# Weight gradients of half the tokens moved beside the forward, kept as fp32 partial sums in DRAM; row sums of a shift gradient as matmuls

## The chip, the cores and the metric

The kernel runs on one core of one Trainium2 chip. The metric is the device time of one execution in microseconds, the median over runs. The engines are TensorE (PE; its weight loads are shown apart as PEld), VectorE (DVE), ScalarE (ACT), GpSimd (POOL) and SyncE (SP, which here only issues DMAs and DMA transposes).

## The reference

One transformer block with adaptive layer norm, forward and backward, on 2048 tokens of width D = 512 (32 heads of 16, MLP width F = 1792), in bf16. Besides the output, the gradients of x, of all weights and of the conditioning vector c are returned.

```python
mod = silu(c) @ w_mod                      # six rows of 512: sa, ca, ga, sb, cb, gb
h = layernorm(x) * (1 + ca) + sa
x = x + ga * attention(h, wqkv, wo)        # full softmax, 32 heads
h = layernorm(x) * (1 + cb) + sb
x = x + gb * (relu(h @ w1 + b1)**2 @ w2 + b2)
out, vjp = jax.vjp(f, x, wqkv, wo, w1, b1, w2, b2, c, w_mod);  grads = vjp(grad_out)
```

The parts that matter here are dW1 = h^T du and dW2 = a^T (gb * g), where du is the gradient at the MLP's first product, a the squared relu and g the output's gradient, and the sums that feed the gradients of cb, sb and gb: products of the unscaled weight gradients with w1 and w2, summed, and db1 @ w1^T for sb.

## The kernel before

The tokens are handled in four chunks of 512 (`SC = 4`), the width of the MLP in 14 tiles of 128 (`FT`), D in four of 128 (`DT`), and the tokens in 16 tiles of 128 (`ST`). The work goes in this order:

1. An opening (`gen_open`, `gen_qkv`) up to 275 us: layer norm, QKV, and the attention of chunk 0.
2. `fwd_rest` (275 to 984 us): the attention of chunks 1 to 3, eight head groups each, 16 key blocks to a group, 384 steps in all. A step has four score matmuls, two exponentials of 128x1024 on ACT and 16 small matmuls into the accumulators. Behind it a `Background` runs generators: `gen_mlp(sc)` is the output projection, the MLP forward and the MLP backward down to dO of chunk `sc`, and it is added to the queue when the attention of that chunk is done. `bg.burst(rate, ...)` gives it a number of units a step (a unit is a matmul of 512 columns); a burst ends where a PSUM tile is finished (`stopped`), and `("wait", n)` lets n/2 steps pass. Slots that are not used are filled by dummy matmuls (line 520).
3. `last_chunk` (984 to 1179 us): the MLP of chunk 3 forward and backward, then both weight gradients over all 16 token tiles. `gen_dw1` makes dW1 in 14 tiles of 64 matmuls with 128 columns, `gen_dw2` makes dW2 in 14 tiles of 16 matmuls with 512 columns. Both need `du` and `a` with tokens on the partitions: for the first three chunks these come by DMA transpose from DRAM (`duT_d`, `aT_d`, written by `gen_mlp`), for the last one from SBUF (`turned`: tiles `tm_blk` and `tm_l`). They are generators as well, and `fill.take(n)` puts n units of them between the steps of the last chunk; the loads for the attention's backward are issued on SP between the units of `gen_dw2`, from its mark `half` on.
4. `attn_bwd` and `phase6` (1179 us to the end): the backward of the attention, and the remaining weight gradients.

PE and SP run in the order of the program. DVE, ACT and POOL are ordered by the compiler's planner in stages 2 and 3. PSUM has eight banks; in `fwd_rest` the background has one (`mps`), in `last_chunk` the gradients have three (`dps`), transposes two (`tps`), everything else three.

In `gen_dw1` DVE makes three passes over each tile piece: the scaled output (line 1110), the product with w1 for cb (line 1112), and the product of `csb` with w1 for sb (line 1115); `csb` is db1 in a row, spread over the partitions by a matmul of ones with a diagonal (lines 1101 to 1103). The marks `fc2_0` to `fc2_2` say how far a chunk's generator has come; `phase_fwd` runs the generator of chunk 2 up to its mark before the last chunk begins, and the rest of it is taken in pieces by `last_chunk` (`bg.take`, `bg.drain`).

## Time and profile before

| what | value |
|---|---|
| median of 3 runs | 2525.01 us (2522.04 to 2526.73) |
| the profiled execution | 2527.3 us, span 2525.3 us |
| granted TensorE clock, mean | 0.994 |
| PE, DVE, ACT, POOL busy | 96%, 67%, 90%, 28% of the span |
| moved by DMA | 454 MB |

A row of groups reads: line, engine, operation, the tile written and the tiles read, the shapes, the count; then the total busy time in us and the mean of one in ns; then the engine's idle time just before them and what ended most of it. A row of the timeline or of the chain starts with the start and the duration in us. A row of stages starts with the stretch, its length, and the busy time (with the count) of PE, PEld, DVE, ACT and POOL, then the granted clock, the busy share of the DMA engines and GB/s. SPq is the queue of SP.

### The profile page before, as it was taken

The page shows a single profiled execution, that of the slowest core. Times are in us where ns is not written, and L with a number is a line of the kernel's source. Part 1 is how long each engine was busy: PE and PEld are TensorE (multiplying, and loading weights), DVE is VectorE, ACT ScalarE, POOL GpSimd, SP SyncE. Part 2 cuts the span into 40 slices and gives each one's busy share as a digit, 9 for nine tenths or more (in the row PEclk, how much of TensorE's full clock was granted, in tenths as well). Part 3 has the DMA queues.
Part 4 walks back from the last instruction along what each step waited for, and adds up shares of the span by engine and source line. Part 5 has one row for each costly group of instructions (what it writes and reads, how often), then busy time and mean ns, then how long its engine had stood idle before and what let it go on. Part 6 is the DMA issues. An engine that isn't in the chain of part 4 may idle for free.

```text
span 2525.3 us, 69141 instructions
## 1 busy us (share of the span) xinstructions
PE 2424.0 (96%) x26994; PEld 1032.7 (41%) x27199; DVE 1683.0 (67%) x3343; ACT 2283.0 (90%) x3757; POOL 715.7 (28%) x1265
## 2 busy tenths in 40 slices
PE   8999999999999999989999999999999999999988
PEld 4555444545554544573232333332333333333333
DVE  6222212322342333576999999999999999999857
ACT  7999999999999996533999999999999999999934
POOL 2344430120121021246222332322332323222323
PEclk9999999999999999999999999999999999999999
DMA  4689650451244054599999999999999999999997
GB/s 166 133 179 209 162 124 22 127 118 48 99 103 100 22 145 120 111 188 214 236 237 226 233 237 232 236 226 228 230 233 234 233 234 234 239 227 238 241 179 188
DMA packets 1291630, 454.19 MB, mean 180 GB/s; under 512 B 1235796, under 2 KB 1260246, under 8 KB 1291302
## 3 DMA queue, kind: packets, MB, share of 16 engines
q1 hardware_dynamic: 1252422, 344.68, 72.4%
q0 software_dynamic: 36800, 104.04, 14.1%
q8 instruction: 212, 3.47, 0.6%
q10 hardware_dynamic: 2080, 1.05, 0.2%
q14 instruction: 116, 0.95, 0.1%
HBM read 75.83 MB, written 64.49 MB: 56 GB/s over the span
## 4 chain that ended last, share of the span: by engine, by line
PE 40%; ACT 8%; DMA 8%; issue 2%; DVE 2%; POOL 0%; SPq 0%; DVEq 0%; ACTq 0%; POOLq 0%
PE st L1710 16%; PE acckv L1561 8%; ACT pu L1713 6%; PE accq L1586 5%; DMA dsT<-ds 4%; PE dps L1151 2%; PE dp L1624 2%; DMA keep<-ds 1%; DMA dqT<-dq_t 1%; ACT csq L1642 1%; PE st L1856 1%; DVE ds L1628 1%; PE dp L1761 1%; PE st L1667 1%; PE st L1574 1%
## 5 line engine op out<-in xcount | busy, mean ns | idle before, releaser
L1628 DVE TENSOR_TENSOR ds<-dp,pu 128x512 bf16<-128x512 f32 x1888 | 1166.8, 684 | 36.5 <-PE dp L1624 20.6
L1713 ACT ACTIVATE pu<-st 128x512 bf16<-128x512 f32 x2048 | 1073.6, 666 | 37.2 <-PE st L1710 21.3
L507 ACT ACTIVATE pu<-st 128x1024 bf16<-128x1024 f32 x768 | 704.9, 1127 | 6.0 <-PE st L503 5.6
L1624 PE MATMUL dp<-kvm,q 64*128 64x512 bf16 x1024 | 364.0, 383 | 2.1 <-DVE ds L1628 1.0
L1624 PE MATMUL dp<-kvm,dOTg 64*128 64x512 bf16 x1024 | 364.9, 384 | 1.0 <-DVE ds L1628 0.8
L1710 PE MATMUL st<-kvm,QTg 64*128 64x512 bf16 x1024 | 348.8, 382 | 6.0
L1710 PE MATMUL st<-kvm,q 64*128 64x512 bf16 x1024 | 347.9, 381 | 5.1 <-ACT pu L1713 0.2
L1643 POOL TENSOR_TENSOR ds<-csq,pu 128x512 bf16<-128x512 f32 x128 | 147.2, 1150 | 626.5 <-ACT csq L1642 547.4
L482 PEld LDWEIGHTS <-pu 128*128 128x128 bf16 x6144 | 216.5, 96 | 158.0 <-issue 83.2
L482 PE MATMUL accbank<-Vaug,pu 128*128 128x17 bf16 x6144 | 265.2, 172 | 10.1 <-ACT pu L507 7.4
L520 PE MATMUL st<-QTm,KTq 128*128 128x512 bf16 x670 | 202.7, 379 | 6.3 <-ACT pu L507 2.7
L413 ACT ACTIVATE pu<-st 128x1024 bf16<-128x1024 f32 x224 | 206.6, 1060 | 2.3 <-PE st L410 1.9
L503 PE MATMUL st<-QTm,KTq 32*128 32x512 bf16 x1536 | 171.9, 385 | 5.2 <-issue 1.0
L1561 PE MATMUL acckv<-ds,Qg 128*16 128x512 bf16 x1024 | 176.5, 383 | 0.2
L1561 PE MATMUL acckv<-pu,dOg 128*16 128x512 bf16 x1024 | 176.4, 383 | 0.0
L1561 PE MATMUL acckv<-ds,q 128*16 128x512 bf16 x1024 | 175.8, 382 | 0.0
L1561 PE MATMUL acckv<-pu,q 128*16 128x512 bf16 x1024 | 175.8, 382 | 0.0
L410 PE MATMUL st<-QTm,KTq 128*128 128x512 bf16 x435 | 130.0, 377 | 10.1 <-ACT pu L413 4.0
L1710 PEld LDWEIGHTS <-q 64*128 64x128 bf16 x1024 | 66.9, 94 | 162.9 <-issue 150.0
L1710 PEld LDWEIGHTS <-QTg 64*128 64x128 bf16 x1024 | 67.1, 94 | 161.5 <-issue 146.5
L347 PEld LDWEIGHTS <-pu 128*128 128x128 bf16 x2048 | 86.4, 96 | 59.6 <-issue 3.0
L1624 PEld LDWEIGHTS <-q 64*128 64x128 bf16 x1024 | 88.8, 93 | 51.3 <-issue 40.8
(399 smaller groups left out, 3365.7 us busy)
## 6 DMA issues: line engine op xcount, KB each, us to landing
KTq<-KTq_d POOLq DMA_DIRECT2D x24, 512.0 KB, 3.8
duT_d<-auT POOLq DMA_DIRECT2D x3, 1792.0 KB, 7.3
aT_d<-rT POOLq DMA_DIRECT2D x3, 1792.0 KB, 11.9
KTq_d<-KTq SPq DMA_DIRECT2D x32, 128.0 KB, 2.2
QTq_d<-ev_fm SPq DMA_DIRECT2D x32, 128.0 KB, 4.4
ktm_d<-ev_tm POOLq DMA_DIRECT2D x32, 128.0 KB, 2.6
VTq_d<-vT POOLq DMA_DIRECT2D x4, 1024.0 KB, 6.1
dx<-dx_d SPq DMA_DIRECT2D x16, 256.0 KB, 4.6
```

The source lines that it names most:

```text
L410: nc.tensor.matmul(stt[:, a, :], lhsT=KT[:, kb * P:(kb + 1) * P], rhs=QTm[2 * jp + a][:], start=True, stop=True)
L413: nc.scalar.activation(pu[:], stt[:], ACT.Exp, scale=self.scale)
L482: nc.tensor.matmul(acc[:, j, sub, :], lhsT=pus[half][:, a, sub * P:(sub + 1) * P], rhs=Vaug[:, kb, 4 * g + j, :], start=(kb == 0 and j == ...
L503: nc.tensor.matmul(tiles[h // 2][:, h % 2, :], lhsT=KT[r, kb * P:(kb + 1) * P], rhs=QTm[g % 2][r, :], start=True, stop=True)
L507: nc.scalar.activation(pu[:], t[:], ACT.Exp, scale=self.scale)
L520: nc.tensor.matmul(tiles[0][:, 0, :], lhsT=KT[:, 0:P], rhs=QTm[g % 2][:], start=True, stop=True)
L1561: nc.tensor.matmul(acckv[r:r + DH, :], lhsT=T[n][:, ib, col:col + DH], rhs=src[:, a, :], start=(ib == 0), stop=(ib == ST - 1))
L1624: nc.tensor.matmul(dp[:], lhsT=T["dOT"][rd, ib * P:(ib + 1) * P], rhs=masked["VT"][a][rd, 512 * c:512 * (c + 1)], start=True, stop=True)
L1628: nc.vector.tensor_tensor(dsg[:, i, a], dp[:], pu[:, a, :], ALU.mult)
L1643: nc.gpsimd.tensor_tensor(dsg[:, i, 1], f[:], pu[:, 1, :], ALU.mult)
L1710: nc.tensor.matmul(stt[:], lhsT=T["QT"][rs, q], rhs=masked["KT"][a][rs, c0:c0 + 512], start=True, stop=True)
L1713: nc.scalar.activation(pu[:, a, :], stt[:], ACT.Exp, scale=self.scale)
```

## The change

The weight gradients of chunks 0 and 1 (`SE` = 8 token tiles) move into the background of the forward. The generator of chunk 1 makes them for chunk 0, that of chunk 2 for chunk 1: `gen_dw2_early` ahead of the first fc2 tile, `gen_dw1_early` behind the second. Each makes 14 tiles of 128x512 from four token tiles. Chunk 0's sums are stored to `dw2p_d` and `dw1p_d` in fp32; chunk 1's passes load them, add, and store again, and the last w1 pass also takes the products with w1 and scales the sum. Buffers are the former `auT` (operand of 4 token tiles, four sums) and the free `QTm[2]`, `QTm[3]`. The rate of the background goes from 3 to 4 units a step, and the mark `fc2_{sc}` moves from behind the first fc2 tile to behind the third. `gen_dw1` and `gen_dw2` then run over the other eight token tiles and add the partial sums: on POOL in the first, on DVE in the second. The row sums for sb become matmuls: each w1 block is transposed on PE, copied by ACT, and multiplied with db1, split into three bf16 parts, into one PSUM tile that stays open for all 14 tiles.

```diff
@@ fwd_rest
-                done = 0 if ... else bg.burst(3.0, self, most)
+                done = 0 if ... else bg.burst(4.0, self, most)
@@ last_chunk
-        xh2 = e0.tile([P, ST, D], BF16, name="xh2")
+        xh2 = e0.tile([P, ST - self.SE, D], BF16, name="xh2")
@@ turned
-            r = pool.tile([P, ST - 4, P], BF16, name="tm_blk", bufs=4)
-            nc.sync.dma_start_transpose(r[:], src_d[ft, :, :(ST - 4) * P])
+            r = pool.tile([P, ST - 4 - SE, P], BF16, name="tm_blk", bufs=4)
+            nc.sync.dma_start_transpose(r[:], src_d[ft, :, SE * P:(ST - 4) * P])
@@ gen_dw1
+        rows = self.dps.tile([P, 512], F32, name="dps")
+        def add_rows(ft):
+            nc.tensor.matmul(rows[0:32, :], lhsT=db1s[:, ft, :], rhs=turnedw[ft][:], start=(ft == 0), stop=(ft == FT - 1))
 ...
-                nc.gpsimd.dma_start(w[:], w1_v[:, :, ft * P:(ft + 1) * P])
+                nc.sync.dma_start(w[:], w1_v[:, :, ft * P:(ft + 1) * P])
+            part = sb.tile([P, DT, P], F32, name="part1", bufs=3)
+            nc.sync.dma_start(part[:].rearrange("p a b -> p (a b)"), self.dw1p_d[ft])
 ...
-                for st in range(ST):
+                for st in range(SE, ST):
 ...
+            tp = self.tps.tile([P, DT, P], BF16, name="tp")
+            for kt in range(DT):
+                nc.tensor.transpose(tp[:, kt, :], w1_blk[:, kt, :], self.ident[:])
+            turnedw.append(sb.tile([P, D], BF16, name="w1T", bufs=2))
+            nc.scalar.copy(turnedw[ft][:], tp[:].rearrange("p a b -> p (a b)"))
+            if ft:
+                add_rows(ft - 1)
             csb_ps = ...
-            dw1 = sb.tile([P, DT, P], BF16, name="dw1")
+            dw1 = sb.tile([P, DT, P], BF16, name="dw1", bufs=3)
             for kt in range(DT):
                 nc.scalar.activation(t1[:, kt, :], csb[:], ACT.Copy, scale=self.mod_col(3)[:, kt:kt + 1])
+            nc.gpsimd.tensor_tensor(t1[:], t1[:], part[:], ALU.add)
+            for kt in range(DT):
 ...
-                nc.vector.scalar_tensor_tensor(junk2[:], csb[:], 1.0, w1_blk[:, kt, :], ...)
@@ gen_dw2
+            part = sb.tile([P, D], F32, name="part2", bufs=4)
+            nc.sync.dma_start(part[:], self.dw2p_d[ft])
 ...
+            nc.vector.tensor_tensor(part[:], pt[:], part[:], ALU.add)
-            nc.vector.tensor_tensor(dw2[:], pt[:], self.mod_row(5), ALU.mult)
+            nc.vector.tensor_tensor(dw2[:], part[:], self.mod_row(5), ALU.mult)
-            nc.vector.tensor_tensor(tmp[:], pt[:], w2_blk[:], ALU.mult)
+            nc.vector.tensor_tensor(tmp[:], part[:], w2_blk[:], ALU.mult)
-            if ft == FT // 2:
+            if ft == 2:
                 yield ("half", 0)
@@ gen_mlp
+            yield from self.gen_dw2_early(sc - 1)          # sc > 0
         yield from fc2(0)
         yield from self.gen_do(sc, *todo.pop(0))
+        yield from fc2(1)
+            yield from self.gen_dw1_early(sc - 1)          # sc > 0
+        yield from fc2(2)
         yield (f"fc2_{sc}", 0)
-        for k in range(1, 4):
-            yield from fc2(k)
+        yield from fc2(3)
+    def gen_dw1_early(self, c):
+        for ft in range(FT):
+            if ft + 2 < FT:
+                self.load_early(c, ft + 2, self.duT_d, self.dw1p_d)     # SP: transpose; if c: load of the sum
+            if last and ft + 1 < FT:
+                load(ft + 1)                                            # POOL: w1 block, two buffers
+            pt = self.mps.tile([P, 512], F32, name="pps")
+            for kt in range(DT):
+                for st in range(4):
+                    nc.tensor.matmul(pt[:, kt * P:(kt + 1) * P], lhsT=self.dw_op[:, st, kt * P:(kt + 1) * P],
+                                     rhs=self.dw_blk[ft % 3][:, st, :], start=(st == 0), stop=(st == 3))
+                self.stopped = kt == DT - 1
+                yield 1
+            s = self.dw_sum[ft % 4]
+            nc.vector.tensor_tensor(s, pt[:], s, ALU.add)               # c == 0: tensor_copy(s, pt[:])
+            if last:
+                for kt in range(DT):
+                    nc.vector.scalar_tensor_tensor(junk[...], s[...], 1.0, blks[ft][:, kt, :], ..., accum_out=self.dcb_e[...])
+                for kt in range(DT):
+                    nc.gpsimd.tensor_scalar(s[...], s[...], self.opcbT[:, kt:kt + 1], 1.0, ALU.mult, ALU.mult)
+            nc.gpsimd.dma_start(self.dw1p_d[ft], s)
```

`gen_dw2_early` has the same form with one matmul of 512 columns for each of the four token tiles, and neither product nor scaling; ahead of it and behind it the operand (`grad_out`, then `xhat2_d`) and the first two blocks are loaded on SP. In `gen_dw2` the diagonal for sb is dropped, and its 32 rows of sums are multiplied with ones directly.

More of the change, by code (lines that the diff above doesn't have):

```diff
@@ L321, in phase_fwd @@
         O32 = self.ra.tile([P, 4, D], F32, name="O32")
-        QTm = [fw.tile([P, 512], BF16, name=f"QTm{j}") for j in range(4)]
+        QTm = self.QTm = [fw.tile([P, 512], BF16, name=f"QTm{j}") for j in range(4)]
         def load_q(qc, g, jp):
@@ L511, in fwd_rest @@
                 most = 5 if held else 2 if kb == 2 and n > 0 else 4
[L512 removed]
+                done = 0 if qc == SC - 1 and f"fc2_{SC - 2}" in bg.seen else bg.burst(4.0, self, most)
                 if pend and not held:
@@ L1053, in get @@
                 lasts.append(t)
-            return [r[:, st, :] for st in range(ST - 4)] + [lasts[-1][:, ft % 4, i, :] for i in range(4)]
+            return [r[:, st, :] for st in range(ST - 4 - SE)] + [lasts[-1][:, ft % 4, i, :] for i in range(4)]
         return get
```

123 lines of the change are left out of this document (95 added, 28 removed).

## Prediction

> **What bounds the kernel now.** I read the page first, then the busy times by stage, then the groups of each stage by shape, the chain of waits where it leaves the forward, and last the DMA issues with their landing times.
>
> ```profile
> span 2525.3 us, 69141 instructions
> L507 ACT ACTIVATE pu<-st 128x1024 bf16<-128x1024 f32 x768 | 704.9, 1127 | 6.0 <-PE st L503 5.6
> core 0: us, PE busy (x) PEld busy (x) DVE busy (x) ACT busy (x) POOL busy (x), PEclk, DMA share, GB/s
> 275.00:984.00 709.00, 683.22 (x9090) 351.84 (x9220) 213.74 (x516) 704.87 (x768) 127.00 (x187) 1.00 0.38 94
> 984.00:1008.50 24.50, 20.24 (x111) 9.78 (x113) 12.03 (x33) 5.67 (x9) 4.71 (x8) 0.93 0.54 188
> 1008.50:1059.90 51.40, 51.08 (x251) 23.40 (x256) 27.15 (x79) 29.68 (x53) 9.78 (x17) 1.00 0.37 83
> 1059.90:1121.30 61.40, 57.70 (x949) 56.88 (x948) 43.46 (x245) 27.06 (x86) 28.53 (x44) 0.97 1.02 188
> 1121.30:1179.40 58.10, 55.26 (x242) 24.70 (x245) 34.89 (x106) 10.54 (x24) 38.40 (x51) 0.97 1.14 239
> ```
>
> The reader is to see three regimes. The forward (275 to 984) is ACT's: 704.9 of 709 us, 384 steps of 1.846 us, one for each group and key block. The weight gradients, w1's from 1059.9 to 1121.3 and w2's from there to 1179.4, are PE's, with DVE and POOL at half to two thirds. Between them lies the last chunk. What follows 1179.4 is not edited; I take it as it is.
>
> **The change, part by part: the forward.** In every step PE has about four 512-column slots beside the attention, filled by background work or, where there is none, by a dummy.
>
> ```profile
> L520 PE MATMUL st<-QTm,KTq 128*128 128x512 bf16 x670 | 202.7, 379 | 6.3 <-ACT pu L507 2.7 <-issue 0.3
> L520 PEld LDWEIGHTS <-KTq 128*128 128x128 bf16 x760 | 61.0, 96 | 40.4 <-issue 5.7
> ```
>
> There are 760 dummies. The change adds 2 chunks x 2 gradients x 14 tiles x 4 = 224 slots and raises the rate from 3 to 4 a step, so they replace dummies: cost nothing on PE while that cover lasts; without it 224 x 0.216 = 48 us. Counting the yields of the generators step by step (the same count gives the 760 of before), chunk 2's w1 pass runs in steps 366 to 381 of 384 and 3 slots are left at the end, so it just fits.
>
> What is not covered is a wait in PE's order: a background matmul that waits holds up the next scores behind it, and PE, busy 683 of these 709 us, has 0.07 us a step to make it good. Four waits are new.
>
> ```profile
> dx_d<-x POOLq DMA_DIRECT2D x4, 256.0 KB, 3.4
> o<-O_d POOLq DMA_DIRECT2D x12, 256.0 KB, 3.2
> L1349 SPq DMA_TRANSPOSE dxT<-dxb x12: 1214/1226/2007, 466.8 to 945.7; - x12
> DMA to landing us min/median/max: 3.2/3.3/3.4
> L1078 POOL TENSOR_SCALAR diag<-ident_f,db x14: 362/377/1004, 1032.4 to 1113.9; 128x128 f32<-128x128 f32 x14
> L1076 POOL DMA_DIRECT2D w_blk<-in_B_w_dram x14: 747/756/812, 1030.9 to 1117.5; - x14
> L1155 POOL DMA_DIRECT2D out_dram<-dw x13 | 7.2, 557 | 9.1 <-DVE dw L1154 9.0
> L1112 DVE SCALAR_TENSOR_TENSOR junk<-dps,w_blk 128x128 bf16<-128x128 f32 x56 | 16.0, 285 | 1.3
> L1154 DVE TENSOR_TENSOR dw<-dps,mod 128x512 bf16<-128x512 f32 x13 | 9.0, 690 | 18.8 <-PE dps L1151 11.1 <-DMA out_dram<-dw 4.8 <-PE dps L1173 3.0
> ```
>
> 1. A block of 128x512 is turned on SP (1.22 us of queue, 3.3 to landing) into one of three buffers, so a tile's transpose starts when the tile three before it is done: (3.3 + 0.9 matmuls + 0.3) / 3 = 1.5 us a tile, under 1.846. Nothing. From 5 us to landing on it would cost.
> 2. In chunk 2 each sum goes DVE add 0.69, POOL store 3.4, SP load 3.2, and four buffers share this: 7.4 / 4 = 1.85 a tile. Break-even; 0 to 5 us over 14 tiles, I take 1. Behind that load on SP wait the next transposes.
> 3. In the last w1 pass POOL also scales the sum in four pieces (4 x 0.377) and issues the w1 block (0.756) and the store (0.557): 2.8 us a tile against 1.846. Tile 13 can be evacuated only after the store of tile 9: first store at 2.7 us, nine tiles of 2.8, then 3.4 + 3.2 + 0.3 make 35 us, against 15 steps or 27: 8 us. DVE needs 0.69 + 4 x (0.285 + 0.082) = 2.2 a tile there, so it isn't the limit. DVE's four products read two SBUF operands while POOL scales; by the row on that below the two hold each other up, at most 4 x 0.367 = 1.5 a tile. I take 0.2 of it, hence 10 us; ends 4 and 23.
> 4. At rate 4, chunk 0's work ends earlier and chunk 1's output projection comes at step 135: 275 + 135 x 1.846 and some 1.5 us into the step, 526 us. Its attention transpose can't start before 517.5, when O_b of that chunk is cast.
>
> ```profile
> 752.29 11.22 SPq L1277 DMA_TRANSPOSE fT<-O_b  x1
> DMA to landing us min/median/max: 19.8/19.8/19.8
> 515.89 1.62 DVE L1262 CAST O_b<-O 128x512 bf16<-128x512 f32 x4
> 292.00:296.00 4.00, 3.95 (x58) 2.02 (x60) 0.00 (x0) 3.88 (x5) 0.00 (x0) 1.00 0.23 79
> ```
>
> Beside the stores of O it took 19.8 us in chunk 2; in chunk 0 it started at 279.7 and all DMA traffic had ended soon after 292. So 8 to 20 us: 0 to 11 us of stall; I take 2, since chunk 1 finds the queues as chunk 0 did, without chunk 2's extra store of dOTq. Forward together: 1 + 10 + 2 = 13 us lost (ends 4 and 39).
>
> **The last chunk.** Only one fc2 tile of chunk 2 is left instead of three, since the mark moves behind the w1 pass.
>
> ```profile
> 997.69 3.51 PE pps L158 x15
> 1001.22 0.70 DVE o L1362
> 1001.97 3.50 PE pps L158 x15
> 1008.51 12.26 PE pps L939 x56
> 999.34 0.81 ACT L924 ACTIVATE xh<-x_l,nmr,rstd 128x512 bf16<-128x512 f32 x1 [1.46 <-DVE nmr L923]
> ```
>
> Both are on the chain (7 us). Behind them waits the normalised chunk, ready at 1000.2; transpose and copy bring the next matmuls to about 1002.5 instead of 1008.5: -6 us (ends -7 and -3, should POOL's backlog delay the x0 loads).
>
> **w1's stage.** PE keeps 448 of 896 matmuls, and gets four transposes, one row-sum matmul and the bias matmuls a tile; DVE loses 56 products with csb. But the row sums hold one of the three PSUM buffers for the whole stage, and POOL's add of the partial now stands ahead of DVE.
>
> ```profile
> 1060.29 1.79 PE dps L1096 x32
> 1155.30 3.45 PE dps L1188 x16
> L1110 DVE SCALAR_TENSOR_TENSOR dw<-dps,opcbT,t 128x128 bf16<-128x128 f32 x56 | 19.4, 346 | 13.1 <-DMA out_dram<-dw 12.6 <-ACT t L1109 0.4
> L1158 POOL TENSOR_TENSOR dgb_acc<-dgb_acc,g2w 128x512 f32<-128x512 f32 x13 | 16.6, 1278 | 0.2
> 1094.21 0.44 PE L1101 MATMUL pps<-diag,ones_f 128*128 128x128 f32 x2
> 1095.26 1.28 ACT L1109 ACTIVATE t<-csb,modT 128x128 f32<-128x128 f32 x4
> 1096.81 0.79 POOL L1118 DMA_DIRECT2D out_dram<-dw  x1 [1.69 <-DVE junk L1115]
> 1131.20 3.58 SPq L1051 DMA_TRANSPOSE tm_l<-rT  x1
> 1175.33 1.85 SPq L1034 DMA_DIRECT2D q<-qtm_d  x4
> ```
>
> On PE alone a tile is 32 x 56 ns = 1.79, plus 4 x 56, one 0.216 and 0.4: 2.6 us. The latency is longer: after a tile's matmuls 0.44 (transposes, row sums), 2.3 from the bias matmul to the end of ACT's four scalings (1094.2 to 1096.5), 1.28 POOL add, 1.4 for DVE's four outputs (its four products fit into the wait), two hand-overs of 0.1: 5.6. With the 1.8 of matmuls a buffer is held 7.4 us; two buffers give 3.7 a tile. With DVE at 2.9 of it, some collisions: 4.0, or 56 us for 14 tiles against 61.4: -5. Lower end PE's, 36 us and 5 for the interleaved chunk work, -20. Upper end: if POOL issues a tile's output store (0.79, waiting for DVE) before the next tile's add, each tile goes through store, diag 0.38, add 1.28 and DVE's eight operations of 0.3 in a row, 4.9 us, 68 us, +7. DVE's 12.6 us of waiting for output stores goes with the third dw1 buffer; next late is the add. SP takes the w1 loads over from POOL and gets the partials: 1.22 + 2 x 0.46 + a quarter of a 3.58 us tm_l, 3.0 a tile, under 4.0.
>
> The start-up splitting of db1 (some ten small DVE operations) is hidden by dx(0), 3 us of PE; without that, 2 us.
>
> **w2's stage.** PE: 112 x 0.216 = 24, with db2 (3.45) and two column matmuls 29 us. DVE: three passes a tile instead of two, 14 x 3 x 0.69 = 29 us, and 10 for the modulation and bias. Two of the three now read both operands from SBUF, beside POOL's 1.28 us add.
>
> ```profile
> 1144.74 0.69 DVE L1182 SCALAR_TENSOR_TENSOR auT<-O,auT 128x512 bf16<-128x512 f32 x1 [0.19 <-ACT O L1175]
> 1145.47 1.79 DVE L1182 SCALAR_TENSOR_TENSOR auT<-O,auT 128x512 bf16<-128x512 f32 x1
> 1145.42 1.28 POOL L1158 TENSOR_TENSOR dgb_acc<-dgb_acc,g2w 128x512 f32<-128x512 f32 x1
> ```
>
> The same DVE operation with two SBUF operands takes 0.69 alone and 1.79 when POOL's add starts 0.05 before it: one after the other. So a tile is 2 x 0.69 + 1.28 = 2.66, with the PSUM pass beside the add: 37 + 10 = 47; SP's sum (14 x 1.68, four tm_l of 3.58, 24 loads of the next phase at 0.46) is 49, of which the first three tiles run ahead. POOL's (1.28 + 0.557 + 0.54 for the w2 block, 2.4 a tile) is lower. I take 48 against 58.1: -10; ends -19 (never met) and -1 (met in full, 3.35 a tile).
>
> The Trainium skill (SBUF — State Buffer, SBUF: two separate sides) says why: a DVE operation with two SBUF inputs and a GpSimd one that reads SBUF take turns on one port pair, for the whole instruction. The trace agrees (1.79 against 0.69). By that rule the last forward pass would also pay in full, the slow rival below.
>
> **Sum.** +13 - 6 - 5 - 10 = -8 us on the profiled 2525.3. That execution took 2527.3 with 2.0 around the span, 2.3 above the median of 2525.0; the median becomes 2517.
>
> **Rivals.**
> Slower: the last w1 pass in the forward. If POOL's scalings and DVE's products exclude each other fully, a tile there costs POOL 2.8 + 1.5 = 4.3 us: 2.7 + 9 x 4.3 + 6.9 = 48 against 27, 21 to 23 us lost instead of 10: -8 + 13 = +5, 2530. The sign turns at 18 us lost, 3.9 us a tile. For: the 1.79 row. Against: half of POOL's 2.8 is DMA issue, in which DVE may run.
> Much faster: both stages follow PE (41 and 29, or -20 and -29), the forward loses 4: -51, 2474. For: PE's 0.94 share of both now. Against: the two buffers and the 1.79 row.
> Even: w1's stage gains nothing (4.4 a tile, POOL's order in part), 2522.
> Not doing what it says: the passes don't fit. At 3 slots over, 0.7 us; the count would have to be wrong.
>
> **How the numbers follow.** Forecast (2500 to 2520) 0.47, much faster 0.15, even (2520 to 2530) 0.17, slower 0.21. The range 2488 to 2538 leaves out about half of the much faster case and the slow case with the long transpose. The likeliest alone: 2500 to 2520. A change under 0.2%, 5 us, can't be told from none here: faster 0.62, same 0.17, slower 0.21.
>
> **What would show it.** Right: L520 down to some 510 weight loads; matmuls at 1.8 us a step until the last 30 us of the forward, where PE idles behind DVE's add and that behind SP's load; one fc2 tile after the forward; in w1's stage PE idle for DVE, 4 us a tile; in w2's stage DVE products over 1 us. Wrong: no gaps at the forward's end; w1's stage at 2.6 or at 4.9 a tile; a late first score after w2's stage because SP's loads are late.

## The result, and the profile after

The changed kernel takes 2552.1 us (median of four, 2546.5 to 2566.1) where the kernel before takes 2525.0: 1.0117 times as long, interval 1.0074 to 1.016. It is slower by 27 us, where 8 us less were forecast, and it lies above the upper end of the range. The profiled execution took 2554.6 us.

First the page's span, then the groups of the exponentials and of the dummies, then the stages, in the columns that the prediction shows for before.

```profile
span 2552.8 us, 69568 instructions
L510 ACT ACTIVATE pu<-st 128x1024 bf16<-128x1024 f32 x768 | 708.1, 1089 | 46.0 <-PE st L506 45.5 <-ACT pu L510 0.4
L523 PE MATMUL st<-QTm,KTq 128*128 128x512 bf16 x513 | 138.0, 381 | 3.8 <-ACT pu L510 3.8
275.00:1026.40 751.40, 705.66 (x9559) 389.48 (x9558) 263.80 (x685) 707.35 (x768) 187.83 (x310) 0.96 0.54 132
1026.40:1043.40 17.00, 13.43 (x87) 6.52 (x88) 11.17 (x32) 5.37 (x8) 5.71 (x11) 1.00 0.67 225
1043.40:1095.00 51.60, 51.60 (x257) 23.46 (x258) 28.38 (x85) 29.95 (x53) 7.78 (x14) 1.00 0.29 77
1095.00:1158.70 63.70, 49.37 (x563) 41.58 (x561) 32.96 (x168) 34.27 (x99) 35.44 (x47) 0.84 0.79 191
1158.70:1213.10 54.40, 39.37 (x145) 14.72 (x144) 43.75 (x83) 10.64 (x22) 37.64 (x50) 0.81 1.04 239
```

| stage, us | before | after | difference | forecast |
|---|---|---|---|---|
| forward, chunks 1 to 3 | 709.0 | 751.4 | +42.4 | +13 |
| up to the last chunk's first fc1 matmul | 24.5 | 17.0 | -7.5 | -6 |
| fc1 to w1's stage | 51.4 | 51.6 | 0 | 0 |
| w1's stage | 61.4 | 63.7 | +2.3 | -5 |
| w2's stage, to the first backward score | 58.1 | 54.4 | -3.7 | -10 |
| from there to the end | 1345.9 | 1339.7 | -6.2 | 0 |

The last row is scatter: in the sixteen traces of this study, with the same code there, the time from the backward's 129th exponential to the end lies between 1254.7 and 1269.5 us, before at 1267.7 and after at 1260.0. Everything that matters is in the first row and in the two stages that did not give what they should.

In the forward ACT was idle 6.0 us before its exponentials; now it is 46.0 us, 45.5 of them behind the scores, that is behind PE, and PE waited behind its background work. The view of waits for 640 to 1030 us says for what; first PE's own, then DVE's and SP's (columns: microseconds, times, longest).

```profile
PE pps L158 <- DMA QTm<-aT_d: 10.2, 6, 3.9
PE pps L1469 <- DMA QTm<-duT_d: 6.5, 3, 3.1
PE pps L158 <- DMA auT<-aT_d: 6.1, 2, 4.5
PE accbank L485 <- DVE O L493: 3.9, 1, 3.9
PE pps L1469 <- DVE auT L1475: 3.2, 5, 1.2
...
DVE lnb_junk L1481 <- DMA x<-in_B_w_dram: 13.5, 8, 4.7
...
SPq L1311 <- DVE o L1396: 22.7, 1, 22.7
...
SPq L1444 <- DMA dw1p_d<-auT: 17.9, 8, 6.1
...
SPq L1444 <- DMA dw2p_d<-auT: 12.1, 8, 5.9
```

QTm, auT <- aT_d and duT_d are the transposed blocks: 22.8 us of PE's waiting, the step that the prediction put at nothing. DVE's 13.5 us are for the w1 blocks of the last pass; one of these waits held up the attention's own division (O), the 3.9 us of `accbank`. SP stood 30 us in front of reloads, each for a store of the same ring buffer to land. How long the transposed blocks took from issue to landing:

```profile
DMA to landing us min/median/max: 2.8/4.4/6.5
```

A last view of the forward is the timeline at two places: the first block of the first w2 pass (it runs in chunk 1's generator and makes chunk 0's gradient), and tiles of the w1 pass behind it.

```profile
658.46 0.52 SPq L1418 DMA_DIRECT2D auT<-in_grad_out_dram  x1
659.03 3.07 SPq L1442 DMA_TRANSPOSE QTm<-aT_d  x2
662.16 1.59 SPq L1442 DMA_TRANSPOSE auT<-aT_d  x1
665.56 0.86 PE L158 MATMUL pps<-auT,QTm 128*128 128x512 bf16 x2 [3.89 <-DMA QTm<-aT_d]
...
712.76 1.05 PE L1469 MATMUL pps<-QTm,auT 128*128 128x128 bf16 x16
...
721.50 1.89 PE L1469 MATMUL pps<-QTm,auT 128*128 128x128 bf16 x16 [3.10 <-DMA QTm<-duT_d]
...
724.30 1.87 PE L1469 MATMUL pps<-QTm,auT 128*128 128x128 bf16 x16
```

The first loads reach SP's queue 3 us before PE needs them. And a wait costs more than itself: the 16 matmuls that take 1.05 us take 1.89 and 1.87 behind a gap of 3.10. In the timeline of ACT the gaps of 4.24 and 3.81 us that these two places cause are each followed by a second one, of 0.59 and 0.84 us, one step on.

Now w1's stage, one turn of the timeline:

```profile
1137.97 0.80 POOL L1142 DMA_DIRECT2D out_dram<-dw  x1
...
1139.41 1.26 POOL L1135 TENSOR_TENSOR t<-t,part 128x512 f32<-128x512 f32 x1 [0.64 <-issue]
...
1140.70 0.35 DVE L1137 SCALAR_TENSOR_TENSOR dw<-dps,opcbT,t 128x128 bf16<-128x128 f32 x1 [4.70 <-POOL t L1135]
...
1142.59 0.08 DVE L1139 DVE_READ_ACCUMULATOR junk<-dps,w_blk 128x1 f32 x1
1142.72 0.38 PE L1114 MATMUL dps<-tm_blk,xh 128*128 128x128 bf16 x4 [2.58 <-DVE junk L1139]
...
1142.76 0.80 POOL L1142 DMA_DIRECT2D out_dram<-dw  x1 [1.73 <-DVE junk L1139]
...
1143.59 1.28 POOL L1135 TENSOR_TENSOR t<-t,part 128x512 f32<-128x512 f32 x1
...
1144.90 0.35 DVE L1137 SCALAR_TENSOR_TENSOR dw<-dps,opcbT,t 128x128 bf16<-128x128 f32 x1 [2.23 <-POOL t L1135]
```

Store issue 0.80, add 1.28, DVE's eight operations 1.97, hand-overs of 0.15: 4.2 us from one tile's first output to the next, and PE waits at the end of it. From w2's stage, groups by shape and two kinds of waits:

```profile
L1183 DVE TENSOR_TENSOR dw<-part,mod 128x512 bf16<-128x512 f32 x14 | 15.3, 1094 | 5.8 <-DMA out_dram<-dw 5.6
L1186 DVE TENSOR_TENSOR part<-part,w_blk 128x512 f32<-128x512 f32 x14 | 12.6, 903 | 0.2
L1181 DVE TENSOR_TENSOR part<-dps,part 128x512 f32<-128x512 f32 x14 | 9.5, 682 | 1.4 <-issue 1.4
...
PE dps L1179 <- DMA tm_blk<-aT_d: 7.3, 4, 2.6
PE dps L1179 <- DMA tm_l<-rT: 5.4, 2, 4.5
...
SPq L1165 <- POOL dgb_acc L1187: 7.0, 6, 2.1
```

The two operations with both operands in SBUF average 1.09 and 0.90 us, the one that reads PSUM 0.68. PE's 15 us of idle time there are mostly transposed blocks, and these stand on SP behind reloads that wait for POOL's add.

### The profile page after: what moved, and what is told of

Its sections match the earlier page's. It is cut to its first block, busy times and chain, and to the rows that moved or that the text cites. A ratio compares the mean times of both kernels' runs of the same rounds, so it can differ in the third digit from the quotient of the medians.

```text
span 2552.8 us, 69568 instructions
## 1 busy us (share of the span) xinstructions
PE 2420.9 (95%) x27022; PEld 1040.8 (41%) x27022; DVE 1737.1 (68%) x3419; ACT 2294.0 (90%) x3768; POOL 786.4 (31%) x1391
## 3 DMA queue, kind: packets, MB, share of 16 engines
q10 hardware_dynamic: 2080, 1.05, 0.2%
## 4 chain that ended last, share of the span: by engine, by line
PE 38%; DMA 8%; ACT 7%; issue 3%; DVE 2%; POOL 1%; SPq 0%; DVEq 0%; ACTq 0%; POOLq 0%
PE st L1827 16%; PE acckv L1678 8%; DMA dsT<-ds 6%; ACT pu L1830 5%; PE accq L1703 5%; PE dp L1741 2%; PE dp L1878 1%; DMA keep<-ds 1%; PE st L1973 1%; DVE ds L1745 1%; ACT csq L1759 1%; PE st L1784 1%; PE dps L1114 1%; PE st L1691 1%; DMA tm_blk<-aT_d 1%
## 5 line engine op out<-in xcount | busy, mean ns | idle before, releaser
L510 ACT ACTIVATE pu<-st 128x1024 bf16<-128x1024 f32 x768 | 708.1, 1089 | 46.0 <-PE st L506 45.5
L416 ACT ACTIVATE pu<-st 128x1024 bf16<-128x1024 f32 x224 | 206.5, 1059 | 1.4 <-PE st L413 1.4
L523 PE MATMUL st<-QTm,KTq 128*128 128x512 bf16 x513 | 138.0, 381 | 3.8 <-ACT pu L510 3.8
L413 PE MATMUL st<-QTm,KTq 128*128 128x512 bf16 x448 | 132.7, 377 | 6.1 <-ACT pu L416 4.0
L1827 PEld LDWEIGHTS <-q 64*128 64x128 bf16 x1024 | 67.0, 94 | 164.5 <-issue 151.3
L1703 PE MATMUL accq<-dsT,keep 128*32 128x256 bf16 x1632 | 105.3, 278 | 5.1 <-DMA dsT<-ds 4.9
## 6 DMA issues: line engine op xcount, KB each, us to landing
dw2p_d<-auT POOLq DMA_DIRECT2D x28, 256.0 KB, 3.9
dw1p_d<-auT POOLq DMA_DIRECT2D x28, 256.0 KB, 4.0
```

Of the source, the lines that this page charges most:

```text
L416: nc.scalar.activation(pu[:], stt[:], ACT.Exp, scale=self.scale)
L510: nc.scalar.activation(pu[:], t[:], ACT.Exp, scale=self.scale)
L523: nc.tensor.matmul(tiles[0][:, 0, :], lhsT=KT[:, 0:P], rhs=QTm[g % 2][:], start=True, stop=True)
L1703: nc.tensor.matmul(accq[r:r + 32, o:o + 256], lhsT=T["K"][:, 4 * c + sub, col:col + 32], rhs=v[:, r // 32 % 2 * 2:r // 32 % 2 * 2 + 2, 4 * ...
L1827: nc.tensor.matmul(stt[:], lhsT=T["QT"][rs, q], rhs=masked["KT"][a][rs, c0:c0 + 512], start=True, stop=True)
```

## The experiments

Three theories were put against each other. A: bytes, the DMA engines are full. B: queues and buffers, that is transposed blocks that come too late, and a ring of four sums with SP in front of it. C, the prediction's: POOL's scaling and DVE's products in the last w1 pass hold each other up.

Two numbers are read from each trace: ACT's idle time in the forward, as in the row above, and the late part, from the end of the last forward exponential to the backward's 129th (before 273.6 us, after 266.5), which includes what the stages leave over for the backward's start. How far they scatter is seen from traces with the same code in the place: the forward of after is also that of e4, e6 and e14, and its idle time is 46.0, 40.9, 49.5 and 47.2; the late part of after, e2, e3 and e10 lies from 266.5 to 271.3. So the four idle times lie 8.6 us apart and the four late parts 4.8, and one trace resolves no less. It helps to split the idle time by the count of the exponentials (768 in the forward): numbers 401 to 520 hold the two passes in chunk 1's generator, 521 to 730 the w2 pass in chunk 2's, with its start, and 731 to 768 the last w1 pass. (e3 and e7 have after's code in the first two columns, so the range of the unchanged code is 6.7 to 11.6 and 14.4 to 18.7 there.)

| ACT idle, us | passes in chunk 1 | w2 pass in chunk 2 | last w1 pass |
|---|---|---|---|
| before | 0 | 0.2 | 0 |
| after | 10.2 | 16.6 | 16.0 |
| the same forward in e4, e6, e14 | 7.9 to 11.6 | 14.4 to 18.0 | 14.6 to 15.9 |
| e1 | 9.0 | 8.8 | 13.5 |
| e2 | 5.9 | 16.1 | 15.1 |
| e3 | 6.7 | 15.6 | 15.7 |
| e5 | 6.1 | 10.9 | 13.1 |
| e7 | 8.6 | 18.7 | 5.6 |
| e10 | 4.9 | 13.6 | 15.2 |
| e8, e12, e13 (one forward) | 0 to 1.1 | 4.3 to 6.9 | 1.1 to 3.4 |
| e9 | 4.1 | 8.2 | 3.1 |
| e11 | 0.9 | 10.5 | 6.7 |

All runs follow in one table, and then one by one.

| run | us, median | ratio to before, interval | ACT idle, forward | late part | w1's stage, us a tile | w2's, us a tile |
|---|---|---|---|---|---|---|
| before | 2525.0 | 1 | 6.0 | 273.6 | 4.71 | 3.68 |
| after | 2552.1 | 1.0117, 1.0074 to 1.016 | 46.0 | 266.5 | 4.84 | 3.78 |
| e1 bf16 sums | 2549.6 | 1.0103, 1.0074 to 1.0133 | 35.5 | 270.0 | 4.87 | 3.65 |
| e2 four blocks | 2554.9 | 1.0142, 1.0102 to 1.0183 | 41.2 | 271.3 | 4.71 | 3.97 |
| e3 quarter of products | 2557.8 | 1.015, 1.0111 to 1.0189 | 42.4 | 270.3 | 4.64 | 3.91 |
| e4 rows on DVE | 2559.4 | 1.0157, 1.0116 to 1.0198 | 40.9 | 265.2 | 4.72 | 3.68 |
| e5 e1, e2, ring of eight | 2542.8 | 1.0081, 1.0056 to 1.0107 | 32.9 | 269.3 | 4.98 | 3.65 |
| e6 store deferred | 2554.5 | 1.0135, 1.0107 to 1.0162 | 49.5 | 266.4 | 4.81 | 3.67 |
| e7 products late | 2537.5 | 1.0056, 1.0034 to 1.0078 | 37.4 | 255.9 | 3.84 | 3.70 |
| e8 all relieved | 2504.7 | 0.9922, 0.9906 to 0.9939 | 8.2 | 258.5 | 3.75 | 3.87 |
| e9 e8, bytes back | 2515.5 | 0.9973, 0.9958 to 0.9987 | 19.0 | 256.0 | 3.73 | 3.77 |
| e10 starts alone | 2548.2 | 1.0108, 1.0081 to 1.0136 | 37.0 | 269.9 | 4.84 | 3.91 |
| e11 e8 with fp32 sums | 2526.3 | 1.0016, 0.9998 to 1.0034 | 20.8 | 256.4 | 3.97 | 3.67 |
| e12 e8, rows on DVE | 2520.5 | 0.9998, 0.9982 to 1.0014 | 11.2 | 265.3 | 4.69 | 3.61 |
| e13 e8, partial on PE | 2503.6 | 0.9926, 0.9902 to 0.995 | 12.9 | 248.2 | 4.11 | 3.25 |
| e14 no gate product | 2553.4 | 1.0124, 1.0092 to 1.0157 | 47.2 | 263.4 | 5.04 | 2.83 |

(us a tile: mean step between the 14 output stores of the stage. Ratios are to runs of the kernel before on the same chip.)

**e1, bf16 sums.**

```diff
-        self.dw1p_d = self.dram("dw1p_d", [FT, P, 512], F32)
-        self.dw2p_d = self.dram("dw2p_d", [FT, P, 512], F32)
+        self.dw1p_d = self.dram("dw1p_d", [FT, P, 512], BF16)
+        self.dw2p_d = self.dram("dw2p_d", [FT, P, 512], BF16)
...
-            nc.vector.tensor_tensor(part[:], pt[:], part[:], ALU.add)
+            tmp = sb.tile([P, D], F32, name="g2w2")
+            nc.vector.tensor_tensor(tmp[:], pt[:], part[:], ALU.add)
...
-        self.dw_sum = [buf[:, o + 512 + 1024 * i:o + 512 + 1024 * (i + 1)].bitcast(F32) for i in range(4)]
+        self.dw_sum = [buf[:, o + 512 + 1024 * i:o + 1024 + 1024 * i] for i in range(4)]
```

> The sums stand in DRAM and in the four ring buffers as bf16, so each store and each reload moves 128 KB instead of 256 KB; the transposes, the buffers, the waits and every instruction count stay. Theory A (the 16 DMA engines are full in chunk 2's passes): between 924 and 958 us of the changed kernel they are busy for 1.00 of the time; a 256 KB transfer is about 0.9 us of all 16 engines and a 128x512 transpose about 0.7, so a tile with store and reload asks for 2.5 us of a step of 1.85; halved it asks for 1.6 and fits. The forward, 42 us longer than before, comes down to 12 to 18 longer, and the stage of w2 loses another 4 to 8 us. Total 2515 to 2530. Theory B (the queue order: three transposed blocks, and SP waiting for a store to land before it reloads a sum): the landing time falls from about 4 to perhaps 3.5, and the forward stays 30 to 40 longer: total 2538 to 2550. Theory C (POOL's scaling and DVE's products hold each other up in the last w1 pass): that pass keeps its 15 us.

Idle 35.5 us instead of 46: 10 us, where A wanted 24 to 30 and B 2 to 12. A alone is excluded, and the gain lies in B's range. It comes mostly in the w2 pass of chunk 2 (8.8 us, against 14.4 to 18.7 with after's code). Half the bytes are worth something there, and most of the loss is something else. The edit has a second effect, in w2's late stage: its add writes a tile of its own, so that SP's reload waits for DVE's add and no longer for POOL's. With both effects PE's 12.7 us of waits for transposed blocks in that stage are gone, and yet it runs at 3.65 us a tile instead of 3.78.

**e2, a fourth transposed block.**

```diff
...
+        for f in range(3) if ft == 0 else [ft + 1] if 1 < ft < self.FT - 1 else []:
-        nc.sync.dma_start_transpose(self.dw_blk[ft % 3], src_d[ft, :, 512 * c:512 * (c + 1)])
+            nc.sync.dma_start_transpose(self.dw_blk[f % 4], src_d[f, :, 512 * c:512 * (c + 1)])
```

> A fourth transposed block, and each transpose issued three tiles ahead instead of two; the sums and their ring stay. Theory B: PE's waits for transposed blocks (22 us of the forward by the weight loads) go, so the forward is 15 to 22 us shorter than in the changed kernel: total 2530 to 2537. Theory A: the bytes are the same; chunk 1's passes (their work asks for 1.6 of 1.85 us) gain what bursts cost, 3 to 6 us, chunk 2's gain nothing: total 2545 to 2552. Theory C: chunk 2's last pass keeps its 15 us.

41.2 us: within the scatter of after's forward, so B's 15 to 22 us are excluded. But what PE waits for has changed, in the same view of waits:

```profile
PE pps L158 <- DMA QTm<-aT_d: 8.5, 2, 4.4
PE pps L158 <- DVE auT L1431: 6.4, 6, 2.6
PE pps L1470 <- DVE auT L1476: 5.7, 7, 1.8
```

Of the waits for blocks the first of each w2 pass are left (and one of 0.8 us); the others went over to the sums: DVE's add, which waits for a reload, which waits on SP for a store. One queue was hidden behind the other.

**e3, a quarter of the products and scalings.**

```diff
-                for kt in range(DT):
+                for kt in range(1):
                     nc.vector.scalar_tensor_tensor(junk[:, kt * P:(kt + 1) * P], s[:, kt * P:(kt + 1) * P], 1.0, blks[ft][:, kt, :],
                                                    ALU.mult, ALU.mult, accum_out=self.dcb_e[:, kt, ft:ft + 1])
-                for kt in range(DT):
+                for kt in range(1):
                     nc.gpsimd.tensor_scalar(s[:, kt * P:(kt + 1) * P], s[:, kt * P:(kt + 1) * P], self.opcbT[:, kt:kt + 1], 1.0,
                                             ALU.mult, ALU.mult)
```

> In the last w1 pass only one of four DVE products and one of four POOL scalings is done (the sums of three quarters of the columns stay unscaled and their column sums are zero); loads, stores and waits stay. Theory C, the prediction's: POOL goes from 2.8 to 1.7 us a tile and the lock is gone; the pass loses 15 us no longer, but 3 or less: total 2538 to 2541. Theory A: with the w1 blocks the pass asks the DMA engines for more than 2.5 us a tile whatever POOL does; it gains 0 to 4 us: total 2548 to 2553.

42.4 us, and 15.7 in the last w1 pass, as without the edit: C's 12 us are excluded. With POOL at 1.7 us a tile instead of 2.8, DVE still waits for the w1 blocks and, now first, for the reloads (waits of DVE, 975 to 1030 us):

```profile
DVE auT L1476 <- DMA auT<-dw1p_d: 11.8, 5, 3.8
...
DVE lnb_junk L1482 <- DMA x<-in_B_w_dram: 6.8, 7, 2.6
```

**e4, the row sums back on DVE.**

```diff
...
-            if ft:
-                add_rows(ft - 1)
...
+                nc.vector.scalar_tensor_tensor(junk2[:], csb[:], 1.0, w1_blk[:, kt, :], ALU.mult, ALU.mult,
+                                               accum_out=dsb_part[:, kt, ft:ft + 1])
```

> The early passes alone: the shift gradient's row sums are back on DVE (four products of csb a tile, no transposes of the w1 block, no row-sum matmul, and the third PSUM buffer is free again); everything of the early passes stays. The forward stays at +42 in every theory. The stage of w1 took 63.7 us with the row sums on TensorE. If the PSUM buffer that the rows hold sets it (the prediction's step), three buffers of 7.4 us give 2.5 a tile and DVE, with its four products of 0.28 more, 4.0: 56 us, total 2544. If POOL's order (store of a tile, then the next tile's add) sets it, DVE's products only lengthen the chain: 64 to 72 us, total 2552 to 2560.

The stage takes 4.72 us a tile instead of 4.84, the late part 265.2 instead of 266.5. With a PSUM buffer more on one side and four DVE operations a tile more on the other, nothing moves. But the pace has another reason now: from 1095 to 1160 us DVE is busy 56.4 of 65 us, where it was 33.1, and it waits 4.1 us for POOL's add, where it waited 25.8. So DVE bounds e4, and the run doesn't tell whether the PSUM buffers bounded after. The third possibility, the ring of store, add and DVE, was not yet shown either.

**e5, bf16 sums, four blocks and a ring of eight.** The edits of e1 and e2, and

```diff
-            s = self.dw_sum[ft % 4]
+            s = self.dw_sum[ft % 8]
```

> bf16 sums again, and the room that they leave is used for a fourth transposed block (issued three tiles ahead) and for eight ring buffers instead of four; the bytes are those of the run with bf16 sums alone. Theory B, now in two parts (a transposed block must land within the two tiles that it is issued ahead; SP stands in front of a reload until a store four tiles older has landed, with the next transposes behind it): with both given more buffers at once, chunk 2's w2 pass loses only its start (4.6 us), and chunk 1's passes together 5; the forward goes from +31 (bf16 sums alone) to +20, the rest being the two starts and the last w1 pass, where DVE waits for w1 blocks of 4.1 us to landing in two buffers: (4.1 + 0.8 + 1.5) / 2 = 3.2 us a tile. Total 2535 to 2542. Theory A (bytes): as with bf16 sums alone, forward +28 to +32, total 2545 to 2552.

32.9 us idle, 2.6 under e1, and a forward 28.6 us longer than before's, where B expected 20 and A 28 to 32: the buffers alone don't do it either. The timeline of ACT shows what is left: the starts of the two w2 passes (gaps of 5.0 and 4.5 us), and in the last w1 pass the division behind a w1 block (3.9) and PE's waits for DVE's adds (eight, 6.3 us).

**e6, the output store behind the next add.**

```diff
             nc.gpsimd.tensor_tensor(t1[:], t1[:], part[:], ALU.add)
+            if ft:
+                store(ft - 1)
...
-                nc.gpsimd.dma_start(dw1_v[:, :, ft * P:(ft + 1) * P], dw1[:])
```

> The changed kernel with one thing moved: in the stage of w1 POOL issues the output store of a tile after the add of the next tile instead of before it. Theory: the stage runs in a ring of store issue 0.80 (waiting for DVE's last product), POOL's add 1.27, DVE's eight operations 1.97, together 4.2 us a tile whatever PE does; with the store out of the ring POOL needs 2.45 a tile and DVE 2.0, and the two PSUM buffers give 3.7: the stage goes from 64 to 55 us, total 2541 to 2546. Rival: the DMA transfers set it (transposes, w1 blocks, partials: 191 GB/s in that stage); then 61 to 64 us, total 2549 to 2554. The forward stays at +37 to +42 in both.

4.81 us a tile. This run tested nothing: POOL's instructions are ordered by the compiler's planner there, and the trace shows store, then add, in nearly the same order as after. It neither speaks for the ring nor against it.

**e7, products late.**

```diff
-        last = 4 * (c + 1) == self.SE
+        last = False
...
-            nc.gpsimd.tensor_tensor(t1[:], t1[:], part[:], ALU.add)
+            u = part
+            nc.vector.tensor_tensor(u[:], g4[:], part[:], ALU.add)
...
-                nc.vector.scalar_tensor_tensor(dw1[:, kt, :], g4[:, kt, :], self.opcbT[:, kt:kt + 1], t1[:, kt, :], ALU.mult, ALU.add)
+                nc.vector.scalar_tensor_tensor(dw1[:, kt, :], u[:, kt, :], self.opcbT[:, kt:kt + 1], t1[:, kt, :], ALU.mult, ALU.add)
```

> The changed kernel without the additional work of the last w1 pass in the forward: no w1 loads, no products, no scalings there. In the late stage DVE adds the partial to the PSUM sum first (one 128x512 operation) and makes outputs and products from it; POOL's add goes. Theory (w1 blocks in two buffers set the last pass, at about 3 us a tile, and DVE standing there holds the attention's own division): chunk 2's w1 pass then loses what its w2 pass loses (some 14 us) instead of 20, forward +33 to +37. In the stage of w1 POOL is out of the ring and DVE needs 0.7 + 4 x 0.35 + 4 x 0.28 = 3.3 a tile: 50 to 56 us instead of 64. Total 2534 to 2542. Rival (bytes): the last pass is relieved of 128 KB of 256-byte rows a tile and gains more, 10 us or over, but the stage of w1, with the same transfers, stays at 61 to 64: total 2538 to 2545.

Idle 37.4 us, 8.6 under after, and 5.6 in the last w1 pass where the unchanged code has 14.6 to 16.0: some 9 to 10 us are what loads, products and scalings of that pass cost together. In the late stage the ring is gone: 3.84 us a tile, the late part 255.9, 10.6 less than after. w1's stage takes 58 us, between the 50 to 56 of the theory and the rival's 61 to 64. Its stages of w1 and w2:

```profile
1087.00:1145.00 58.00, 46.54 (x581) 37.83 (x579) 45.06 (x206) 37.36 (x107) 23.35 (x38) 0.92 1.06 225
1145.00:1190.00 45.00, 34.11 (x126) 12.71 (x128) 40.91 (x55) 7.70 (x15) 32.30 (x44) 0.87 0.99 264
```

DVE is busy 45 of 58 us in spite of 9.5 us more work, and POOL's add no longer stands ahead of it. As the transfers are the same as in after, they were not what held w1's stage at 4.8. The edit also frees a PSUM buffer after one DVE operation instead of eight; e13 below separates the two.

**e10, the start alone.** The first loads of a w2 pass are issued ahead of an fc2 tile:

```diff
-            yield from self.gen_dw2_early(sc - 1)
+            early = self.gen_dw2_early(sc - 1)
+            yield next(early)
         yield from fc2(0)
+        if sc:
+            yield from early
```

> The changed kernel with the start alone mended: the first loads of each early w2 pass are issued before an fc2 tile of 15 slots, not 3 steps ahead of the first matmul. The first wait of each w2 pass (4.2 and 4.6 us, and 0.6 to 0.9 behind each) goes; nothing else does. Forward +30 to +34 instead of +37 to +42, total 2540 to 2546. Rival: the first blocks come as late as before, since SP stands behind other waits (22.7 us at one store of a chunk): no change, total 2548 to 2554.

37.0 us, 9 less than after, and a forward 33.5 us longer than before's, as expected; of the 3.9 us for the very first block there is 0.5 left, and the second w2 pass starts without a wait. The total doesn't show it: 2548.2 us is in the rival's range, 2548 to 2554, and the ratio's interval overlaps after's.

**e8, all relieved.** The edits of e5, e7 and e10 together.

> All of it: bf16 sums, four transposed blocks, eight ring buffers, products late, and the first loads of each early w2 pass issued before an fc2 tile of 15 slots instead of right ahead of the pass. Theory B: nothing is left that PE waits long for in the forward; it ends 5 to 10 us later than before's, the last chunk gives 6, the stage of w1 5 to 10: total 2512 to 2525, the first version not slower than before. Theory A (bytes): bf16 brings 10 and the w1 loads 5 to 10: 2530 to 2537.

```profile
L510 ACT ACTIVATE pu<-st 128x1024 bf16<-128x1024 f32 x768 | 706.0, 1116 | 8.2 <-PE st L506 7.7 <-ACT pu L510 0.4
```

The forward is 2 us longer than before's, with the same matmuls in it as after: the slots were free, as the prediction had counted. The version takes 0.9922 of before's time, 20 us less in the median. Its profiled execution was the slowest of its four, 2514.6 us where the others lie from 2502.2 to 2505.6; in it, 12.5 us shorter than before's, the late part gives 15 us and the forward costs 2.

**e9, the bytes back.**

```diff
             nc.gpsimd.dma_start(self.dw2p_d[ft], s)
+            for i in range(1 + min(c, 1)):
+                nc.gpsimd.dma_start(self.dwx_d[i, ft], s)
...
```

The same stands behind the store to `dw1p_d`.

> The version with everything relieved (2504.7 us, forward 2 us longer than before's), to which the bytes of fp32 sums are given back as transfers that nothing reads: in chunk 1's passes each bf16 sum is stored twice, in chunk 2's three times, so that store and reload move 256 and 512 KB a tile again. Blocks, ring and reloads are as they were. Theory A (the DMA engines are full: 2.5 us of all 16 for a tile in a step of 1.85): chunk 2's two passes lose 9 us each, the forward comes to +18 to +25, total 2520 to 2530. Theory B (waits of a queue, not bytes): eight ring buffers and three tiles of lead take it; forward +2 to +8, total 2504 to 2511.

**e11, the same with fp32 sums** (the edits of e2, e7 and e10).

> Everything relieved but with fp32 sums, so the ring has four buffers again (there is no room for more). Theory B: the ring is what is left: a sum's add 0.7, store 4, reload 3.5 and waits make 8 us, over four buffers 2.0 to 2.6 a tile where 1.85 are given: 8 to 12 us in each of chunk 2's passes, forward +17 to +24, total 2519 to 2528. Theory A gives the same bytes as the run with the bytes put back, and so the same time as that one, whatever it is. If the run with the bytes is fast and this one slow, it is the ring; if both are slow, the bytes; if both are fast, neither.

The exponentials of e9, then of e11; then the stretch from 925 to 955 us in after, e8, e9 and e11, in this order.

```profile
L511 ACT ACTIVATE pu<-st 128x1024 bf16<-128x1024 f32 x768 | 707.0, 1104 | 19.0 <-PE st L507 18.2 <-ACT pu L511 0.4
```

```profile
L510 ACT ACTIVATE pu<-st 128x1024 bf16<-128x1024 f32 x768 | 706.9, 1105 | 20.8 <-PE st L506 20.2 <-ACT pu L510 0.4
```

```profile
925.00:955.00 30.00, 20.93 (x224) 10.23 (x221) 6.84 (x12) 18.55 (x21) 6.50 (x12) 0.79 1.03 231
```

```profile
925.00:955.00 30.00, 26.86 (x378) 15.61 (x382) 9.81 (x20) 26.70 (x30) 7.43 (x13) 0.94 0.82 185
```

```profile
925.00:955.00 30.00, 23.21 (x276) 12.13 (x281) 9.05 (x15) 22.61 (x26) 18.37 (x35) 0.83 0.98 248
```

```profile
925.00:955.00 30.00, 24.31 (x294) 12.81 (x296) 9.88 (x21) 22.22 (x24) 7.99 (x15) 0.89 1.01 263
```

Where the DMA engines are busy 0.82 of the time ACT works 26.7 of 30 us; where they are full it does not, whether the bytes are read by anyone or not. Against the three relieved forwards (8.2, 11.2 and 12.9 us in e8, e12 and e13) the bytes cost 6 to 11 us, less than A's 16 to 23. POOL issues three stores a tile in e9 instead of one, which is a second difference; e11, with one store, comes to 20.8 and bounds it. Bytes and a ring of four together cost 8 to 13 us of idle time; the ring by itself is not resolved in the traces. The totals say more: with ten executions each on one chip, e9 takes 2515.5 us and e11 2526.3, and the intervals of their ratios don't overlap. So fp32 sums, with a ring of four and twice the bytes of partial sums in the late stages, cost some 11 us beyond the transfers that e9 puts back. Where, stays open: of the 7.7 us between the two profiled executions 1.4 lie in the forward, 0.3 in the late part and 6.0 in the backward, whose code is the same.

**e12, e8 with the row sums on DVE** (the edit of e4 on e8).

> The version with everything relieved, but with the shift gradient's row sums back on DVE: four products of csb a tile, no row-sum matmuls, and the third PSUM buffer free. With the partial added on DVE that engine is the stage's bound: 0.7 + 4 x 0.35 + 4 x 0.36 = 3.5 us a tile with the rows on TensorE, and 4 x 0.36 = 1.4 more without; the stage of w1 goes from 53 to 64 to 70 us, total 2514 to 2522. Rival: with three PSUM buffers and DMA as the bound the stage stays within 4 us: total 2503 to 2509.

4.69 us a tile instead of 3.75, late part 265.3 instead of 258.5. In the window of w1's stage (1059 to 1127 us) DVE is busy 62 of 68:

```profile
1059.00:1127.00 68.00, 43.73 (x519) 36.63 (x519) 62.21 (x315) 28.87 (x92) 23.68 (x39) 0.85 0.77 175
```

The same edit that changed nothing in e4 costs 7 us in the late part once POOL's add is out of the way.

**e13, the partial on TensorE** (on e8; the same in w2's stage with one matmul of 512 columns).

```diff
...
-            u = sb.tile([P, DT, P], F32, name="u1", bufs=1)
-            nc.vector.tensor_tensor(u[:], g4[:], part[:], ALU.add)
+                nc.tensor.matmul(g4[:, kt, :], lhsT=self.ident[:], rhs=part[:, kt, :], start=False, stop=True)
...
```

Outputs and products then read the sum in PSUM.

> The version with everything relieved, but the partial no longer takes a DVE operation in the two late stages: TensorE adds it to the PSUM sum by a matmul with the identity (four of 128 columns a tile in the stage of w1, one of 512 in that of w2), and outputs and products are made from PSUM. Theory (DVE bounds the late stages: 46.4 of 58 us, then 38.6 of 45, and 80 of 88 in the first backward stretch behind them): 14 operations of 0.7 us in each stage go, and in the stage of w2 two of three DVE operations read PSUM again and need not take turns with POOL's add; from the forward's end to the 128th score of the backward it takes 8 to 16 us less than the 258.5 of the relieved version. Total 2490 to 2498. Rival (the transfers bound them: 0.96 to 0.98 of the DMA engines): the same bytes, no change within 3 us, total 2502 to 2508.

The late part falls by 10.3 us to 248.2, as expected, but not where it was expected in full: w2's stage and the backward's start give it (3.25 us a tile for 3.87; the first 128 exponentials 78.9 us for 87.4), while w1's stage is slower, 4.11 for 3.75. There DVE now waits 17.9 us for ACT's scalings, which stand right ahead of it. For the ring of after it says more than e7: here a tile keeps its PSUM buffer through all eight DVE operations again, POOL's add is gone, and the stage runs at 4.11 instead of 4.84. The bf16 sums aren't the reason, for with them alone it takes 4.87 (e1). In this execution the forward, whose code is e8's, was idle 12.9 us for 8.2, and the median, 2503.6, is not to be told from e8's. The total misses its expectation and lies in the rival's range.

**e14, no gate product** (on after).

```diff
+            if ft == 0:
-            nc.vector.tensor_tensor(tmp[:], part[:], w2_blk[:], ALU.mult)
-            nc.gpsimd.tensor_tensor(dgb[:], dgb[:], tmp[:], ALU.add)
+                nc.vector.tensor_tensor(tmp[:], part[:], w2_blk[:], ALU.mult)
+                nc.gpsimd.tensor_tensor(dgb[:], dgb[:], tmp[:], ALU.add)
```

> The changed kernel, where in the stage of w2 only the first of 14 tiles makes the product of the sum with w2 and POOL's add into the gate gradient (the rest of that sum is left out); loads and waits for them stay. Theory of the prediction (2.66 us a tile: two DVE operations and POOL's add take turns): one DVE operation and the add less leaves 1.4 a tile, so PE's 29 us or the transfers come next; the stage goes from 54 to 42 to 46 us and the first backward stretch is 3 to 6 us shorter. Total 2536 to 2545. Rival (transposes and reloads on SP bound it: PE waits 15 of the 54 us for transposed blocks, with 1.04 of the DMA engines busy): the stage stays at 50 to 55; total 2546 to 2553.

w2's stage goes from 3.78 to 2.83 us a tile, 12 us in 13 steps, and the operation that took turns with POOL's add comes down from 1094 ns:

```profile
L1183 DVE TENSOR_TENSOR dw<-part,mod 128x512 bf16<-128x512 f32 x14 | 10.0, 716 | 9.2 <-DMA out_dram<-dw 9.1
```

So in after DVE's product and POOL's add did set that stage. (The run takes away SP's wait for that add as well; by e1 that wait is worth little.) The total does not follow, and 2553.4 us is just above the rival's range: the planner laid the last chunk's work differently, w1's first store came 6 us later after the forward's end and its stage took 5.04 a tile, so that the late part is only 3 us shorter.

## Why the prediction was wrong

**The slots.** 513 dummies of the forecast 510, and with the waits relieved the forward costs 2 us in e8: PE time was free. That step was right, and it was not the question.

**The forward: +13 (4 to 39)**, measured +42.4, above its own upper end. The text looked for gaps in the last 30 us alone. It put the passes in chunk 1 at nothing and chunk 2's w2 pass at 0 to 5 us at most, and ACT was idle 10.2 and 16.6 us there. Steps 1 and 2 failed.

**Step 1, the transposes: "Nothing".** This step failed. It took 3.3 us to landing from a transpose of before's forward, where the DMA engines are busy 0.38 of the time, though the text itself set the limit: from 5 us on it would cost. Beside the transfers that the change itself adds, the landing is 4.4 us in the median and up to 6.5. And it reckoned with blocks in steady flow, not with the first one: the start of each w2 pass was in no term, since the loads are written ahead of the first matmul in the code; but SP reached them 3 us before it. Measured: 9 us for the starts (e10). The fourth block by itself is not resolved (e2): 5.9 us in the passes of chunk 1, where the unchanged code has 6.7 to 11.6, and no gain in chunk 2's, where the ring takes over.

**Step 2, the ring: 1 us, "0 to 5 us over 14 tiles".** This step failed too. Break-even was reckoned with landings of 3.4 and 3.2 us. What was not counted is bytes: store and reload are 512 KB a tile of 1.85 us, and in chunk 2's passes the DMA engines are at 1.00 to 1.03 where ACT stands. Bytes and ring together cost 8 to 13 us of ACT's idle time (e11 against the relieved forwards), bytes alone 6 to 11 (e9). The forecast forward contains no DMA sum at all; the row of w1's stage of before, 1.02 at 188 GB/s, could have warned.

**Step 3, the last w1 pass: +10.** Its size was nearly right, 8.6 us (e7), its mechanism was not: three quarters of the products and scalings less leave the pass at 15.7 us of idle time (e3). What the trace shows is a w1 block of 4.1 us to landing in two buffers, loaded one tile ahead, and DVE in front of it with the attention's division behind. No run takes the w1 loads away alone.

**Step 4: +2**, measured 0.5 (one wait for fT<-O_b).

These terms, 9, 8 to 13 and 8.6, make 26 to 31 us; the relieved forwards are idle 33 to 38 us less than after's. Some 2 to 12 us are not assigned to one cause; the waits take each other's place, as e2 showed.

**The last chunk: -6**, measured -7.5. Right.

**w1's stage: -5**, measured +2.3. The chain of 5.6 us over two buffers was not the bound. The case that the text named as the upper end was: POOL issues a store, which waits for DVE, before the next tile's add. It was put at 4.9 a tile and is 4.2 where nothing else lies between, 4.84 in the mean. e13 and e7 show that the add is what counts, since without it the stage runs at 4.11 with the PSUM buffers held as before and at 3.84 with them freed early. What the row sums gave on TensorE could not appear as long as that ring stood: without them DVE alone gives 4.72 a tile (e4), hardly less than the ring's 4.84. When the ring was gone it did appear (e12).

**w2's stage: -10**, measured -3.7, or -2.2 if the backward's start is taken in (77.8 us for 128 exponentials before, 79.3 after). The mechanism was the forecast one, DVE and POOL taking turns (1.09 and 0.90 us for operations that take 0.69 alone), and e14 shows its weight. Mis-sized was the rate, 3.78 instead of about 3.4 a tile. SP's reload waits for POOL's add to free its buffer, with the next transposes behind, but that link is not the reason: where the reload waits for DVE's add instead, the stage still runs at 3.65 (e1, e5) or 3.87 (e8). DVE's three operations cost 2.67 us a tile, the collisions included, as forecast. What the sum left out is what DVE waits for in after's stage: 5.6 us for output stores to land, and 5.4 for POOL's add of w1's last tiles. That is read from the trace; no run took these waits away. The Trainium skill (SBUF — State Buffer, SBUF: two separate sides) says that such operations exclude each other for a whole instruction; the trace agrees, with maxima of 2.07 and 1.80 us.

**The rivals.** The slower rival had the right sign but the wrong mechanism, POOL and DVE in the last pass, and its 2530 is 22 us short. The even one had POOL's order in w1's stage, at 4.4 a tile, and nothing of the forward. The much faster one is refuted: PE waits 15 us in each late stage.
